# Two key loads cut at partition 68, longer rows of wo, and the last value sums behind the last scores, in a decode kernel on one core

## The chip, the cores and the metric

The kernel runs on one core of a Trainium2 chip. The metric is the device time of one execution in microseconds (us); of several executions the median is quoted. A comparison always uses a new kernel and the kernel before on the same chip in the same rounds.

## The reference, cut to what matters

One token (`x`, 640 values) passes a layer with attention over a long cache and a small feed-forward part.

```python
H, Sk, Dh = 32, 32768, 192
q = (layernorm(x) @ wq).reshape(1, 1, H, Dh)
scores = einsum("bhqd,bhkd->bhqk", q, k_cache) * Dh ** -0.5
p = softmax(scores)
o = einsum("bhqk,bhkd->bhqd", p, v_cache)
h = x + o.reshape(1, 1, H * Dh) @ wo
out = h + relu(layernorm(h) @ w1) @ w2
```

Keys and values are 2 x 32 x 32768 x 192 bf16 numbers, 805 MB, and each is used once. The rest is small: 825 MB are read in all.

## The kernel before

Keys and values come in 130 loads each. A usual load puts 64 keys on each of the 128 partitions: 128 rows of 24,576 bytes. The last head ends with short loads (40, 16 and 8 keys per partition, numbers 127, 128 and 129). All loads are issued from one queue, into three buffers for keys and three for values.

```python
def load_part(ld, src, pool, tag, name):
    h, k0, jl = loads[ld]
    ...
    t = pool.tile([P, size], bf16, tag=tag, name=name)
    nc.sync.dma_start(out=t[:, 0:jl * Dh],
                      in_=src[h, k0:k0 + P * jl, :].rearrange("(p j) d -> p (j d)", p=P))
    return t

wo_view = A_wo.rearrange("(b p) n -> p b n", p=P)
def load_wo(pr):                                   # once for each pair of heads
    t = wop.tile([P, 3, D], bf16, name="wo")
    nc.sync.dma_start(out=t[:], in_=wo_view[:, 3 * pr:3 * pr + 3, :])   # rows of 1280 bytes
```

Each load is worked on in chunks (32 keys per partition in the usual case). Of a chunk, TensorE transposes 20 keys per partition and forms their scores (`transposes`, `scores_pe`); VectorE does the other 12 with a multiplication and a sum (`scores_dve`); ScalarE takes the exponentials (`pB` and `pA`). The sum over values, `pv`, is a row of matmuls with `pA` or `pB` as weights. It runs one chunk later, behind the next chunk's transposes, so that TensorE has work while ScalarE copies the transposed keys.

```python
for g in range(G):
    ...                                            # issue loads
    transposes(g)
    if g > 0:
        pv(g - 1)
    scores_pe(g)
    sc = scores_dve(g)
    ...                                            # once per head: den, o_scale, o_turn, project, next q
    exp_dve(g, sc)
den_mm(H - 1); den_rec(H - 1)
pv(G - 1)
o_scale(H - 1); o_turn(H - 1); project(H // 2 - 1)
...                                                # layernorm, feed-forward, store
```

`o_scale` divides a head's sums by the softmax denominator, and `o_turn` puts two heads' results on partitions with 12 instructions on TensorE (six f32 matmuls, each recorded as two):

```python
nc.tensor.matmul(ps[:, b:b + 1], lhsT=src[:, i, b * P:(b + 1) * P], rhs=ident_f[0:2, i:i + 1], ...)
```

The softmax here doesn't subtract the row's maximum and nothing guards it: scores larger than these inputs give would overflow.

## Time and profile before

| kernel before | |
|---|---|
| time, median of 3 | 1954.45 us (1954.04 to 1954.61) |
| DMA bytes and mean rate | 827.85 MB, 424 GB/s |
| TensorE, VectorE, ScalarE busy | 82%, 69%, 55% |
| one 24,576-byte row on one DMA engine | 912 ns |
| 159 instruction fetches (queue q8) | spread over eight of the 16 engines by the prediction's count, 1.42 us lost in the one that was followed |

The lines that carry this stand in the prediction. To read them: the row of nines is the mean busy share of the 16 DMA engines in 40 slices of the span, and the row below it is what they moved. Both are flat until the last slice, so the stream of loads sets the time. The waits view of the kernel before says the same from the other side (columns: waiting engine, tile and line, what it waited for, us in total, times, longest):

```profile
DVE pr L266 <- DMA kt<-in_A_k_cache_dram: 479.9, 126, 8.8
PE tp L239 <- DMA kt<-in_A_k_cache_dram: 269.7, 119, 5.4
```

### The profile page before, as it was taken

How to read it: one execution, taken by the hardware profiler on the slowest of the kernel's cores; microseconds unless marked ns; L12 is line 12 of the kernel's file. 1: busy time of each engine (PE TensorE's matmuls, PEld its weight loads, DVE VectorE, ACT ScalarE, POOL GpSimd, SP SyncE). 2: the span in 40 equal slices, each digit the busy share in tenths (PEclk: the TensorE clock that was granted, in tenths of full speed). 3: DMA queues.
4: the chain of work that ended last, by engine and by line, in shares of the span. 5: the costliest groups of instructions: out<-in, count | busy, mean ns of one | idle time of the engine just before them, and what ended most of it. 6: DMA issues, size and time to landing. Idle time of an engine off the chain costs nothing.

```text
span 1952.3 us, 44906 instructions
## 1 busy us (share of the span) xinstructions
PE 1594.4 (82%) x20392; PEld 1122.4 (57%) x20392; DVE 1338.0 (69%) x654; ACT 1067.5 (55%) x2223; POOL 0.7 (0%) x6
## 2 busy tenths in 40 slices
PE   6887887878788788787888877888788887887887
PEld 4655565555556556555555655655555565565655
DVE  5766777667666676676767666777666766676675
ACT  4555555555555555555655555555555555555554
POOL 0000000000000000000000000000000000000000
PEclk9989889989998889998988989899899989898998
DMA  9999999999999999999999999999999999999996
GB/s 405 431 429 429 430 431 430 429 429 431 431 430 428 430 431 430 431 429 431 430 429 430 429 431 430 430 431 424 431 431 428 425 421 431 427 430 426 430 421 253
DMA packets 51522, 827.85 MB, mean 424 GB/s; under 512 B 4612, under 2 KB 17412, under 8 KB 18564
## 3 DMA queue, kind: packets, MB, share of 16 engines
q1 hardware_dynamic: 51332, 824.99, 99.0%
q8 instruction: 159, 2.61, 0.5%
q14 instruction: 31, 0.25, 0.0%
HBM read 824.97 MB, written 0.00 MB: 423 GB/s over the span
## 4 chain that ended last, share of the span: by engine, by line
DMA 77%; PE 17%; ACT 4%; DVE 1%; issue 1%; SPq 0%; ACTq 0%
DMA kt<-in_A_k_cache_dram 75%; PE o_ps L293 8%; PE tp L239 6%; ACT kT L240 3%; DMA vt<-in_A_v_cache_dram 1%; DVE pr L266 1%; PE sp L249 1%; PE sp L253 1%; PE sp L251 1%; PE qps L205 0%; ACT pA L276 0%; ACT pB L256 0%; DVE o_pair L314 0%; PE oT_ps L327 0%; ACT row_e L208 0%
## 5 line engine op out<-in xcount | busy, mean ns | idle before, releaser
L240 ACT COPY kT<-tp 128x1024 bf16<-128x1024 bf16 (+1 forms) x1025 | 905.2, 966 | 343.1 <-PE tp L239 340.2
L266 DVE TENSOR_TENSOR pr<-kt,qb 128x2304 f32<-128x2304 bf16 (+1 forms) x258 | 655.0, 2539 | 483.3 <-DMA kt<-in_A_k_cache_dram 479.9
L239 PE MATMUL tp<-ident_b,kt 128*128 128x128 bf16 x7677 | 599.3, 242 | 342.8 <-DMA kt<-in_A_k_cache_dram 269.7
L239 PEld LDWEIGHTS <-kt 128*128 128x128 bf16 x7677 | 531.1, 110 | 381.2 <-DMA kt<-in_A_k_cache_dram 280.2
L269 DVE TENSOR_REDUCE sc<-pr 128x12 f32<-128x2304 f32 (+1 forms) x258 | 654.3, 2536 | 27.6 <-ACT kT L240 1.4
L293 PE MATMUL o_ps<-vt,pB 128*2 128x384 bf16 x2559 | 498.8, 346 | 2.6 <-DMA vt<-in_A_v_cache_dram 2.6
L293 PEld LDWEIGHTS <-pB 128*2 128x2 bf16 x2559 | 203.8, 87 | 226.9 <-issue 65.9
L256 ACT ACTIVATE pB<-sp 128x20 bf16<-128x20 f32 (+1 forms) x258 | 48.4, 188 | 492.4 <-PE sp L253 492.4
L293 PE MATMUL o_ps<-vt,pA 128*2 128x384 bf16 x1537 | 291.9, 326 | 0.0
L249 PEld LDWEIGHTS <-kT 128*128 128x128 bf16 x2559 | 196.1, 96 | 85.7 <-issue 84.7
L249 PE MATMUL sp<-qm,kT 128*128 128x2 bf16 x2559 | 218.6, 164 | 0.5 <-ACT kT L240 0.5
L251 PE MATMUL sp<-qm,kT 128*128 128x1 bf16 x2559 | 215.0, 163 | 0.0
L253 PE MATMUL sp<-qm,kT 128*128 128x1 bf16 x2559 | 215.0, 163 | 0.0
L251 PEld LDWEIGHTS <-kT 128*128 128x128 bf16 x2559 | 198.7, 96 | 0.0
L293 PEld LDWEIGHTS <-pA 128*2 128x2 bf16 x1537 | 129.1, 84 | 120.8
L253 PEld LDWEIGHTS <-kT 128*128 128x128 bf16 x2559 | 197.4, 96 | 0.0
L276 ACT ACTIVATE pA<-sc 128x12 bf16<-128x12 f32 (+1 forms) x258 | 52.8, 205 | 0.0
L256 ACT ACTIVATION_READ_ACCUMULATOR pB<-sp 128x1 f32 x258 | 50.1, 194 | 0.0
L276 ACT ACTIVATION_READ_ACCUMULATOR pA<-sc 128x1 f32 x258 | 49.3, 191 | 0.0
L305 DVE TENSOR_REDUCE rec<-den 128x1 f32<-128x20 f32 x32 | 5.7, 179 | 60.2 <-PE den L299 60.2
L315 ACT ACTIVATE o_pair<-o_ps,rec 2x192 f32<-2x192 f32 x32 | 13.2, 412 | 26.9 <-DVE o_pair L314 26.9
L327 PE MATMUL oT_ps<-ident_f,o_pair 2*128 2x1 f32 x192 | 24.2, 247 | 0.1
(60 smaller groups left out, 191.4 us busy)
## 6 DMA issues: line engine op xcount, KB each, us to landing
kt<-in_A_k_cache_dram SPq DMA_DIRECT2D x127, 3072.0 KB, 35.7
vt<-in_A_v_cache_dram SPq DMA_DIRECT2D x127, 3072.0 KB, 31.4
wq<-in_A_wq_dram SPq DMA_DIRECT2D x8, 960.0 KB, 34.7
wo<-in_A_wo_dram SPq DMA_DIRECT2D x16, 480.0 KB, 31.2
kt<-in_A_k_cache_dram SPq DMA_DIRECT2D x1, 1920.0 KB, 30.7
vt<-in_A_v_cache_dram SPq DMA_DIRECT2D x1, 1920.0 KB, 25.4
kt<-in_B_w_dram SPq DMA_DIRECT2D x1, 1920.0 KB, 17.1
vt<-in_B_w_dram SPq DMA_DIRECT2D x2, 960.0 KB, 13.3
```

The lines of the kernel that those rows point to most:

```text
L239: nc.tensor.transpose(out=tp[:, b, :], in_=kt[:, off:off + P], identity=ident_b[:])
L240: nc.scalar.copy(out=kT[:, b0:b0 + nb, :], in_=tp[:, 0:nb, :])
L249: nc.tensor.matmul(sp[:, 2 * i:2 * i + 2], lhsT=kT[:, 3 * i + 1, :], rhs=qm[:, 1:3], start=True, stop=False, skip_group_check=True)
L251: nc.tensor.matmul(sp[:, 2 * i:2 * i + 1], lhsT=kT[:, 3 * i, :], rhs=qm[:, 0:1], start=False, stop=False, skip_group_check=True)
L253: nc.tensor.matmul(sp[:, 2 * i + 1:2 * i + 2], lhsT=kT[:, 3 * i + 2, :], rhs=qm[:, 3:4], start=False, stop=True, skip_group_check=True)
L256: nc.scalar.activation(out=pB[:, 0:JP], in_=sp[:, 0:JP], func=F.Exp, scale=SCALE, accum_out=dsums[:, h, 2 * c + 1:2 * c + 2])
L266: nc.vector.tensor_tensor(out=pr[:, 0:JD, :], in0=kt[:, c0 * Dh:(c0 + JD) * Dh].rearrange("p (j d) -> p j d", d=Dh), in1=qb[:].unsqueeze(1 ...
L269: nc.vector.reduce_sum(out=sc[:, 0:JD], in_=pr[:, 0:JD, :], axis=mybir.AxisListType.X)
L276: nc.scalar.activation(out=pA[:, 0:JD], in_=sc[:, 0:JD], func=F.Exp, scale=SCALE, accum_out=dsums[:, h, 2 * c:2 * c + 1])
L293: nc.tensor.matmul(o[:], lhsT=p, rhs=vt[:, (c0 + j) * Dh:(c0 + j + 2) * Dh], start=first, stop=last)
L315: nc.scalar.activation(out=dst[:, 1, n0:n0 + Dh], in_=o[:, Dh:2 * Dh], func=F.Copy, scale=s[0:2, 1:2])
L327: nc.tensor.matmul(ps[:, b:b + 1], lhsT=src[:, i, b * P:(b + 1) * P], rhs=ident_f[0:2, i:i + 1], start=(i == 0), stop=(i == 1))
```

## The change

Its intent, as the change itself suggests it: eight DMA engines are some 20 us behind the other eight at the end, as by the prediction's count they also carry the instruction fetches (1.42 us lost in the one that was followed). So it moves rows from engines 4 to 15 to engines 0 to 3 in two loads (60 and 117), makes the rows of `wo` three times longer, and takes the last value sums out of the way of the last scores.

```diff
+    few = (15 * len(loads) // 32, 29 * len(loads) // 32)
+    ENDS = [g for g in range(G) if chunks[g][2] >= len(loads) - NEND]
-    pcp = ... bufs=3
+    pcp = ... bufs=6
-    wo_view = A_wo.rearrange("(b p) n -> p b n", p=P)
+    wo_view = A_wo.rearrange("(g p b) n -> g p b n", p=P, b=3)
-        nc.sync.dma_start(out=t[:], in_=wo_view[:, 3 * pr:3 * pr + 3, :])
+        nc.sync.dma_start(out=t[:], in_=wo_view[pr])
-        nc.sync.dma_start(out=t[:, 0:jl * Dh], in_=src[h, k0:k0 + P * jl, :].rearrange(...))
+        rows = src[h, k0:k0 + P * jl, :].rearrange("(p j) d -> p (j d)", p=P)
+        for j0, j1 in parts or [(0, jl)]:
+            for p0, p1 in [(0, 68), (68, P)] if ld in few and name == "kt" else [(0, P)]:
+                nc.sync.dma_start(out=t[p0:p1, j0 * Dh:j1 * Dh], in_=rows[p0:p1, j0 * Dh:j1 * Dh])
...   (the value loads of the last head's end pass parts: one transfer per chunk)
-                    nc.tensor.matmul(ps[:, b:b + 1], lhsT=src[:, i, b * P:(b + 1) * P], ...)
+                    nc.tensor.matmul(ps[:, b:b + 1], lhsT=src[:, i, b:3 * P:3], ...)
-            if g > 0:
+            if g > 0 and g - 1 not in ENDS:
                 pv(g - 1)
...
         den_rec(H - 1)
-        pv(G - 1)
+        for g in ENDS:
+            pv(g)
```

More of the change, by code (lines that the diff above doesn't have):

```diff
@@ L79 @@
     scp = ctx.enter_context(tc.tile_pool(name="scp", bufs=3))
-    pcp = ctx.enter_context(tc.tile_pool(name="pcp", bufs=3))
+    pcp = ctx.enter_context(tc.tile_pool(name="pcp", bufs=6))
     small = ctx.enter_context(tc.tile_pool(name="small", bufs=2))
@@ L112, in load_wo, with load_part @@
         t = wop.tile([P, 3, D], bf16, name="wo")
-        nc.sync.dma_start(out=t[:], in_=wo_view[:, 3 * pr:3 * pr + 3, :])
+        nc.sync.dma_start(out=t[:], in_=wo_view[pr])
         wo_t[pr] = t
-    def load_part(ld, src, pool, tag, name):
+    def load_part(ld, src, pool, tag, name, parts=None):
         h, k0, jl = loads[ld]
@@ L122, in load_part @@
         t = pool.tile([P, size], bf16, tag=tag, name=name)
-        nc.sync.dma_start(out=t[:, 0:jl * Dh], in_=src[h, k0:k0 + P * jl, :].rearrange("(p j) d -> p (j d)", p=P))
+        rows = src[h, k0:k0 + P * jl, :].rearrange("(p j) d -> p (j d)", p=P)
+        for j0, j1 in parts or [(0, jl)]:
+            for p0, p1 in [(0, 68), (68, P)] if ld in few and name == "kt" else [(0, P)]:
+                nc.sync.dma_start(out=t[p0:p1, j0 * Dh:j1 * Dh], in_=rows[p0:p1, j0 * Dh:j1 * Dh])
         return t
@@ L129, in load_v @@
     def load_v(ld):
-        vt_t[ld] = load_part(ld, v_hd, vpool, "vt", "vt")
+        parts = [(q[3], q[3] + q[4]) for q in chunks if q[2] == ld] if ld >= len(loads) - NEND else None
+        vt_t[ld] = load_part(ld, v_hd, vpool, "vt", "vt", parts)
     w_t = {}
@@ L326, in o_turn @@
                 for i in range(2):
-                    nc.tensor.matmul(ps[:, b:b + 1], lhsT=src[:, i, b * P:(b + 1) * P], rhs=ident_f[0:2, i:i + 1],
+                    nc.tensor.matmul(ps[:, b:b + 1], lhsT=src[:, i, b:3 * P:3], rhs=ident_f[0:2, i:i + 1],
                                      start=(i == 0), stop=(i == 1))
```

## The prediction

> **What bounds the kernel now.** I read the page first (parts 2, 3, 4, 6), then the sync queue's and TensorE's lines of the timeline at the end, then the single DMA packets and semaphore landings that the trace keeps.
>
> ```profile
> span 1952.3 us, 44906 instructions
> DMA  9999999999999999999999999999999999999996
> GB/s 405 431 429 429 430 431 430 429 429 431 431 430 428 430 431 430 431 429 431 430 429 430 429 431 430 430 431 424 431 431 428 425 421 431 427 430 426 430 421 253
> q1 hardware_dynamic: 51332, 824.99, 99.0%
> q8 instruction: 159, 2.61, 0.5%
> ...
> DMA 77%; PE 17%; ACT 4%; DVE 1%; issue 1%; SPq 0%; ACTq 0%
> ...
> kt<-in_A_k_cache_dram SPq DMA_DIRECT2D x127, 3072.0 KB, 35.7
> ...
> wo<-in_A_wo_dram SPq DMA_DIRECT2D x16, 480.0 KB, 31.2
> ```
>
> The row of 9s and the flat 430 GB/s say that the transfers run without a pause until the last slice; the chain puts 77% on DMA. TensorE is busy 82% of the span but waits for keys (the waits view gives 269.7 us of it at the transposes). So only two things can move the time: the DMA stream, or the last 40 us after it.
>
> The stream has a grain that the page doesn't show. In the packet records a 24,576-byte row occupies an engine for 912 ns, and its successor starts 4 ns before its end: 908 ns a row, 27.1 GB/s, times 16 is 433 GB/s. So every engine runs at its pace all the time. But the 16 engines don't finish a load together. From the landings of each load, sorted: at 109 us eight landings are within 0.8 us of the first and eight are 1.7 to 1.8 us late; at 920 us (load 61) eight are 12.9 to 14.6 us late; from 1350 us on they are some 20 us late, and the gap stops growing. Of the early eight, six agree within 1.1 us, one is 1 to 4 us late, one 4 to 8.
>
> The cause is in the packets of q8: 159 instruction fetches of 16,384 bytes. Following rows of equal phase shows that they fall on eight engines in a fixed rotation. One example, 22.5 us into the span: the fetch takes 932 ns, in which its engine carries no row, and the next row takes 1411 ns instead of 912; the engine loses 1.42 us. 159/8 = 19.9 fetches per engine x 1.42 = **28.2 us** for each of eight engines; the gap's growth (14 us in 910 us, so 29 over 1924) agrees. A load is finished by its latest engine, so these eight set the time. The gap stays at 20 us since the early ones run out of issued loads.
>
> **The end.**
>
> ```profile
> 1893.43 12.61 SPq L123 DMA_DIRECT2D kt<-in_A_k_cache_dram  x3
> 1906.10 13.78 SPq L123 DMA_DIRECT2D vt<-in_A_v_cache_dram  x3
> ...
> 1912.12 3.38 PE L239 MATMUL tp<-ident_b,kt 128*128 128x128 bf16 x30 [3.39 <-DMA kt<-in_A_k_cache_dram]
> ...
> 1931.56 1.14 PE L293 MATMUL o_ps<-vt,pB 128*2 128x384 bf16 x6 [0.76 <-DMA vt<-in_A_v_cache_dram]
> ...
> 1937.27 0.97 PE L293 MATMUL o_ps<-vt,pB 128*2 128x384 bf16 x5
> ...
> 1939.51 0.40 PE L299 MATMUL den<-dsums,ones_mat 128*128 128x20 f32 x2 [0.54 <-ACT pA L276]
> 1939.84 0.49 PE L293 MATMUL o_ps<-vt,pB 128*2 128x384 bf16 x2
> ```
>
> The last real wait for the stream is the one for load 126, at 1912.1 (3.39 us). From there TensorE and ScalarE work through six chunks one after the other, with a single wait of 0.76 us for values. Loads 127, 128 and 129 of the keys are on the chip by 1924.1, 1926.0 and 1927.0, their values by 1931.5, 1933.4 and 1934.4. The value sums end at 1940.66, and 11.6 us of small steps follow.
>
> [...]
>
> **The change, part by part.**
>
> *68/60 split, key loads 60 and 117 (15/32 and 29/32 of 130).* Usual share 8 rows per engine. New: engines 0 to 3 get 17+4 = 21 (+13), 4 to 14 get 4 (-4), 15 gets none (-8). Over two loads: +26 rows on 0 to 3 = +23.6 us, -8 rows = -7.3 us on 4 to 14. This makes sense if engines 0 to 3 carry no fetches and the eight late ones lie in 4 to 15. I infer that from the change's numbers, since 23.6 against 28.2-7.3 = 20.9 is nearly a balance; the trace can't confirm it. Then the end is set by engines 0 to 3: 28.2-23.6 = **4.6 us earlier**. On the way: at load 60 they lead by 14 us and lose 17 rows = 15.4 us against the late ones, so they fall 1.5 us behind them; by load 117 they lead by 11.5 and fall 4 behind. That is far inside the 20 us of queue.
>
> *wo rows.* Per engine and load, 24 packets of 1280 bytes become 8 of 3840. Start to start 1280 takes 51.8 ns; 3840, between 3072 (121 recorded) and 6144 (234), about 149-4 = 145 ns. 24 x 51.8 = 1.24 us against 8 x 145 = 1.16; times 16 loads = **1.3 us earlier**. The strided ident matmuls (6 per pair of heads) I take as free.
>
> *Last scores first.* Chunks A, B (load 127), C, D lose their value sums from between the scores and get them after the denominator. Worked in the times of before: scores of A end at 1929.8; ScalarE's copies for B end at 1932.55, and the scores of B needn't wait for A's sums: exponentials at 1933.1 instead of 1933.9. C: copies 1933.7 to 1935.5, exponentials from 1936.0 (was 1936.95). D: its copy ends 1937.3, exponentials to 1938.05 (was 1939.46), denominator to 1938.5. Then all 10+10+8+4 = 32 sums stand behind it, at 1.78 us for ten: 5.3 us, to 1943.8, where they ended at 1940.66. So this costs **3.1 us**: it takes sums out of time in which TensorE waited for ScalarE, to avoid a wait for values of 0.76 us. The load of v 127 in two parts and pcp with 6 buffers gain nothing, as all values have landed by then.
>
> Sum: -4.6 - 1.3 + 3.1 = -2.8 us: 1951.6; I say 1951.
>
> **Rivals.**
> - [...] the 19 us that 21 rows take become up to 38, twice: engines 0 to 3 would then end up to 33 us after the present end (23.6+38-28.2): about 1988[...]. [...] Against: nothing in the trace; an amount so near a balance looks tuned by measurement.
> - *Wrong engines.* If one of the eight with fetches is among 0 to 3, it keeps 28.2 and gets 23.6: 1954.45+23.6-1.3+3.1 = 1980. [...] (the early engine that is up to 8 us late, some 10 by the end): 23.6+10-28.2 = +5.4, so 1962.
> - *The new order doesn't cost*, if the clock or ScalarE lets TensorE run the sums sooner than I think: 1948 to 1949.
> - *More from the stream:* if the latest engine loses all of its 7.3 us: also 1948 to 1949.
>
> **Range and chances.** Half of my weight is on 1947 to 1954, some 15% below it or in small variants, a third on contention or wrong engines, spread over 1955 to 1990. So 1944 to 1977 for 8 in 10. Faster by over 2% (below 1915) is out of the stream's reach; slower by over 2% (above 1993) needs full contention: 4%.
>
> **What would show it.** Right: the sorted landings of load 60 have four late engines, within 3 us of the other late ones; the gap of the eight is near zero after it, grows to some 11 us by load 117 and ends within 4 us; load 126 lands near 1906; TensorE then runs 32 sums in a row of 5.3 us behind the denominator, ending 3 us later after load 126's landing than now. Wrong: rows over 912 ns in number around load 60 (contention), or gaps of over 20 us after it (wrong engines), with TensorE waiting for keys in the middle of the run.

The sum: -4.6 - 1.3 + 3.1 = -2.8 us, 1951.6, said as 1951. Its first term supposes that 68 rows go to four engines and 60 rows to fifteen. The first rival, called contention in what follows, supposed that rows of different engines get in each other's way, so that one takes up to twice its time.

## The result, and the profile after

| | kernel before | changed kernel |
|---|---|---|
| time, median of 4 | 1954.24 us (1953.99 to 1954.61) | 2028.53 us (2026.11 to 2030.18) |
| ratio, 95% interval | | 1.0379 (1.0361 to 1.0397) |

The changed kernel is 3.8% slower.

The page of the changed kernel, its span, DMA rows, queue and key loads (the last group: tile and source, queue, operation, count, KB each, us from issue to landing):

```profile
span 2025.8 us, 44915 instructions
...
DMA  9999999999999999999999999999999999998994
GB/s 406 431 430 429 430 430 430 428 430 432 430 431 430 429 431 430 430 371 270 428 431 430 426 429 430 431 431 429 429 431 431 425 430 429 431 228 311 431 404 170
...
q1 hardware_dynamic: 47386, 824.99, 97.9%
...
kt<-in_A_k_cache_dram SPq DMA_DIRECT2D x125, 3072.0 KB, 35.4
...
kt<-in_A_k_cache_dram SPq DMA_DIRECT2D x2, 1440.0 KB, 73.9
```

The last line is the 60-row part of the cut loads: 73.9 us from issue to landing, where a usual key load takes 35.4. The bytes are the same as before, the packets fewer (47,386 against 51,332: longer `wo` rows). What is new is in two places of the GB/s row, around 900 us and 1800 us, where the two cut loads are: 371 and 270, then 228 and 311, in place of 430. And the row of nines above doesn't move at the first of them. **The engines are as busy as ever and move half as much.** The engine shares alone would have hidden it.

The size of the loss can be read off that row. A slice is 2025.8/40 = 50.6 us. Against 430 GB/s the slices of 371 and 270 lose 50.6 x (59 + 160)/430 = 25.8 us, and those of 228 and 311 lose 50.6 x (202 + 119)/430 = 37.8 us: 64 us together, of the 74 that the kernel got slower.

A closer look: the windows view of the kernel before, then of the changed kernel, around the first cut load (columns: stretch, length, busy time and instructions of each engine, TensorE's granted clock, DMA share, GB/s):

```profile
890.00:898.50 8.50, 8.50 (x104) 6.54 (x102) 8.26 (x4) 5.15 (x11) 0.00 (x0) 0.81 1.01 433
898.50:905.50 7.00, 4.37 (x59) 2.63 (x56) 1.63 (x1) 3.68 (x10) 0.00 (x0) 1.00 0.99 424
```

```profile
890.00:898.50 8.50, 8.24 (x97) 5.79 (x95) 8.26 (x4) 5.52 (x12) 0.00 (x0) 0.80 1.05 424
898.50:905.50 7.00, 4.20 (x57) 2.56 (x56) 1.24 (x1) 3.25 (x9) 0.00 (x0) 1.00 1.01 211
...
915.00:930.00 15.00, 9.19 (x86) 5.04 (x84) 5.91 (x3) 4.22 (x9) 0.00 (x0) 0.80 1.05 204
930.00:943.00 13.00, 1.27 (x32) 0.86 (x30) 0.00 (x0) 0.47 (x4) 0.00 (x0) 0.63 0.97 206
```

The rate falls at 898.5 us, at once, and stays at half for some 45 us, at a DMA share near 1. In the DMA records no row that starts between 899 and 942 us takes under 1665 ns, and the median of these 357 rows is 1854. The last columns are the ones to compare; in the last stretch the compute engines have run out of keys.

The waits view of the changed kernel:

```profile
DVE pr L274 <- DMA kt<-in_A_k_cache_dram: 529.8, 115, 39.5
PE tp L247 <- DMA kt<-in_A_k_cache_dram: 303.4, 112, 31.5
```

These are 49.9 us and 33.7 us more than before, in fewer waits, and the longest grew from 8.8 to 39.5 us: the new wait sits in one or two places.

Following the landings of single loads against the kernel before: the values of load 58 land at about the same time (0.4 us sooner), load 60 is complete 29.9 us late, the delay has shrunk to 22 us by load 115, is 70 us when load 117 is complete, 67 to 68 us for the last values, and 73 us at the output. So each cut costs tens of microseconds, and the end costs another five. At the second cut there is more: when the slow rows are through, the engines have nothing left to do, since the computation had starved and freed no buffers. The windows view of the changed kernel shows it as a share below one:

```profile
1830.00:1840.00 10.00, 0.00 (x0) 0.00 (x0) 0.00 (x0) 0.00 (x0) 0.00 (x0) 0.50 0.76 307
1840.00:1850.00 10.00, 3.12 (x30) 3.12 (x30) 3.02 (x2) 2.01 (x3) 0.00 (x0) 0.50 0.58 236
```

TensorE's timeline at the end of the changed kernel (start, length, engine, line, operation, tiles, shapes, count, idle time before and its releaser), to be held against the tail in the prediction:

```profile
2004.61 0.62 PE L307 MATMUL den<-dsums,ones_mat 128*128 128x20 f32 x2 [0.54 <-ACT pA L284]
2005.16 2.08 PE L301 MATMUL o_ps<-vt,pB 128*2 128x384 bf16 x6
2007.03 1.48 PE L301 MATMUL o_ps<-vt,pA 128*2 128x384 bf16 x4
...
2012.16 0.49 PE L301 MATMUL o_ps<-vt,pA 128*2 128x384 bf16 x2
```

The value sums do stand in one row behind the denominator, as planned. But the first six take 2.08 us, where six took 1.14 us in the kernel before, and the row lasts from 2005.16 to 2012.65, 7.5 us instead of the 5.3 that the prediction had worked out.

### The profile page after: what moved, and what is told of

It is laid out like the page before. It is cut to its first block, busy times and chain, and to the rows that moved or that the text cites. A ratio compares the mean times of both kernels' runs of the same rounds, so it can differ in the third digit from the quotient of the medians.

```text
span 2025.8 us, 44915 instructions
## 1 busy us (share of the span) xinstructions
PE 1619.3 (80%) x20392; PEld 1137.7 (56%) x20392; DVE 1336.9 (66%) x654; ACT 1067.3 (53%) x2223; POOL 0.7 (0%) x6
## 3 DMA queue, kind: packets, MB, share of 16 engines
q1 hardware_dynamic: 47386, 824.99, 97.9%
## 4 chain that ended last, share of the span: by engine, by line
DMA 73%; PE 18%; ACT 4%; another core or an unknown queue 2%; DVE 2%; issue 1%; SPq 0%; ACTq 0%
DMA kt<-in_A_k_cache_dram 68%; PE o_ps L301 9%; PE tp L247 6%; DMA vt<-in_A_v_cache_dram 5%; ACT kT L248 3%; DVE pr L274 1%; PE sp L257 1%; PE sp L261 1%; PE oT_ps L335 1%; PE sp L259 1%; DVE o_pair L322 0%; ACT pA L284 0%; ACT pB L264 0%; PE den L307 0%
## 5 line engine op out<-in xcount | busy, mean ns | idle before, releaser
L301 PE MATMUL o_ps<-vt,pB 128*2 128x384 bf16 x2559 | 508.7, 350 | 13.1 <-DMA vt<-in_A_v_cache_dram 13.0
L335 PE MATMUL oT_ps<-ident_f,o_pair 2*128 2x1 f32 x192 | 36.4, 312 | 0.5 <-DVE o_pair L322 0.5
L335 PEld LDWEIGHTS oT_ps<-ident_f,o_pair 2*128 2x128 f32 x192 | 35.0, 258 | 1.2 <-DVE o_pair L322 0.9
## 6 DMA issues: line engine op xcount, KB each, us to landing
kt<-in_A_k_cache_dram SPq DMA_DIRECT2D x125, 3072.0 KB, 35.4
kt<-in_A_k_cache_dram SPq DMA_DIRECT2D x2, 1440.0 KB, 73.9
vt<-in_A_v_cache_dram SPq DMA_DIRECT2D x2, 960.0 KB, 23.6
```

The lines of the kernel that those rows point to most:

```text
L301: nc.tensor.matmul(o[:], lhsT=p, rhs=vt[:, (c0 + j) * Dh:(c0 + j + 2) * Dh], start=first, stop=last)
L335: nc.tensor.matmul(ps[:, b:b + 1], lhsT=src[:, i, b:3 * P:3], rhs=ident_f[0:2, i:i + 1], start=(i == 0), stop=(i == 1))
```

## The experiments

All kernels are the kernel before with one edit, except "no_split", which is the changed kernel with one edit, and "wo_perm" and "parts_wo", which join two. All gave correct results. The "two theories" of the expectations are contention and overloaded engines (too many rows on engines 0 to 3). "Rows" are the durations of 24,576-byte packets in the trace's DMA records.

| run | what it does | median us | ratio to before (95%) |
|---|---|---|---|
| no_split | the change without the cut loads | 1958.97 | 1.0022 (1.0009 to 1.0036) |
| split_only | the cut loads alone | 2021.91 | 1.0347 (1.0332 to 1.0361) |
| wo_only | the wo rows alone | 1954.66 | 1.0000 (0.9987 to 1.0012) |
| order_only | the new order alone | 1959.23 | 1.0023 (1.0011 to 1.0036) |
| halves_64 | the two loads cut at partition 64 | 1996.91 | 1.0216 (1.0199 to 1.0233) |
| columns | the two loads cut along the row | 1955.15 | 1.0001 (0.9986 to 1.0016) |
| markers | 16 tiny transfers, to number the engines | 1955.77 | one run |
| spread | the cut in small doses | 2010.99 | 1.0286 (1.0271 to 1.0302) |
| block16 | eight transfers of 16 neighbouring rows | 1990.18 | 1.0182 (1.0168 to 1.0195) |
| stride16 | eight transfers of every eighth row | 1985.13 | 1.0156 (1.0142 to 1.0170) |
| own8 | eight-row transfers, each engine in its usual partitions | 1974.29 | 1.0100 (1.0085 to 1.0116) |
| foreign8 | the same, each engine in partitions of another | 1991.95 | 1.0185 (1.0170 to 1.0200) |
| dram_perm | full width, rows read elsewhere in memory | 1954.82 | 0.9999 (0.9982 to 1.0015) |
| wo_perm | long wo rows, no strided weights | 1954.59 | 1.0001 (0.9989 to 1.0014) |
| order_warm | the new order, TensorE kept busy | 1956.72 | 1.0011 (0.9997 to 1.0025) |
| parts_wo | wo_perm and the end's values in parts | 1953.63 | 0.9989 (0.9975 to 1.0003) |

The medians of the kernel before in the same rounds lay between 1954.34 and 1955.07.

### Which part of the change costs the time

**no_split** sets the list of cut loads to nothing:

```diff
-    few = (15 * len(loads) // 32, 29 * len(loads) // 32)
+    few = ()
```

> The changed kernel with the 68/60 split alone taken out (wo rows and late value sums stay). If the split carries the loss [...], the 74 us vanish and what is left is the rest of the change: -1.3 us for wo, +3.1 us for the order, so 1956 us and the last key load lands as before. If the late value sums cost much more than I worked out, 1960 us or more.

**split_only** puts the cut alone into the kernel before:

```diff
+        if name == "kt" and ld in (60, 117):
+            for p0, p1 in [(0, 68), (68, P)]:
+                nc.sync.dma_start(out=t[p0:p1, 0:jl * Dh], in_=rows[p0:p1, 0:jl * Dh])
```

> The kernel before with the 68/60 split of key loads 60 and 117 alone. Both theories: some 2022 to 2027 us, with the landings of load 60 delayed by 30 us and rows of 1.8 and 2.7 us around it. If the split needs the other parts to do harm, less than 2000 us.

Measured: 1958.97 (4.3 us above the kernel before of its rounds, 1954.65) and 2021.91 (67.3 above). Together 71.6, of the 74.3 that the whole change costs; 2.7 us are not put down to either, but the four runs of split_only lie between 2019.77 and 2026.98, so these 2.7 us are not clear of noise. So the cut loads are the cause, and their delay is there in split_only at the same loads: 30.2 us at load 60 and 68.0 at load 117, measured at the landing of each.

### Wrong engines, or slow rows

The prediction's two serious rivals were that engines 0 to 3 are not the early ones, and that the rows get slow. **markers** sends one tiny transfer of n rows for each n from 1 to 16 in the middle of the run; each has n landings. The trace has no engine numbers, so an engine is numbered here by the first of these transfers that lands on it: the landing that is new with each n belongs to engine n-1. That the 68 rows of a cut load go to the first four of this numbering is an assumption, but it fits: in the changed kernel they are through at 931.6, 931.9, 936.8 and 942.4 us, two together and two later, as engines 0 and 2, then 3 and 1 are below.

```diff
+    marks = [const.tile([16, 16], bf16, name=f"mark{n}") for n in range(1, 17)]
+    def mark(n):
+        nc.sync.dma_start(out=marks[n - 1][0:n, :], in_=A_wo[0:n, 0:16])
...
+            if 16 <= h < 20 and c in (2, 3, 5, 6):
+                mark(4 * (h - 16) + {2: 1, 3: 2, 5: 3, 6: 4}[c])
```

> The kernel before with 16 tiny transfers of 1 to 16 rows of 32 bytes, four in each of heads 16 to 19, to learn engine numbers: a transfer of n rows lands on n engines, each when its queue gets there. [...] engines 0 to 3 are early ones (the transfers of 1 to 4 rows land early, 14 us or more ahead of the late eight), so the loss isn't from fetches on them. Wrong engines: at least one of the first four landings is 13 us or more late. Time as before within 2 us.

Engines 0, 2, 7, 8 and 15 are the early ones. Behind them, 4 is 1.0 to 1.9 us late, 3 is 3.3 to 4.4 and 1 is 5.6 to 7.3; why, no run shows. The eight late ones, 14 to 19 us, are 5, 6 and 9 to 14. So the prediction's inference that none of the eight is among engines 0 to 3 was right, and the first rival falls in its main form. Its milder form, an engine among the four that is up to 8 us late, holds: that is engine 1.

The rows decide for the second. Durations of all rows that start between 900.5 and 904.5 us, from the DMA records (not a view of the profile):

```
kernel      rows   shortest  median  longest (ns)
before        70        912     912       912
after         38       1766    1866      2446
split_only    35       1752    1865      2088
halves_64     33       1636    1942      2329
own8          55        912     912       912
foreign8      31       1833    1876      1922
block16       35       1718    1780      2007
stride16      33       1849    1924      1991
```

Twice the time per row, and not only on engines 0 to 3. At that moment the early engines have reached the cut load. The eight late ones, 14 us behind, are still on the loads before it, with 128 partitions as always, and one engine, 15 by this numbering, has no row of the cut load at all (fifteen landings for the 60 rows, and the four of the 68 rows are among them: 938.8, 939.2, 944.1 and 950.0 us, 7.2 to 7.6 us after the first four). **Every one of their rows is slow too**; the shortest in the changed kernel and in split_only is 1752 ns.

### What about the cut makes rows slow

**halves_64** cuts at 64, which gives every engine its usual number of rows, 4 + 4, if 64 rows go to 16 engines as 128 do (16 landings for a usual load). **columns** cuts each row in two, which makes two transfers as well, but both on 128 partitions. The 1.8 us a row in the expectation of halves_64 are twice the usual 908 ns, an assumption. The 5 ns for a packet in that of columns are an estimate: a 1280-byte packet takes 51.8 ns from start to start in the kernel before, and 1280 bytes at 27.1 GB/s alone would take 47.2.

```diff
+            for p0, p1 in [(0, 64), (64, P)]:                        # halves_64
+                nc.sync.dma_start(out=t[p0:p1, 0:jl * Dh], in_=rows[p0:p1, 0:jl * Dh])
```
```diff
+            for c0 in (0, jl * Dh // 2):                             # columns
+                nc.sync.dma_start(out=t[:, c0:c0 + jl * Dh // 2], in_=rows[:, c0:c0 + jl * Dh // 2])
```

> The kernel before, key loads 60 and 117 as two transfers of 64 rows, each on 16 engines, 4 rows each. No engine gets more than its 8 rows. [...] rows of 1.8 us, 7.3 us longer per load, 10 to 15 us slower in all. Overloaded engines (the amount of rows on engines 0 to 3 alone does it): no difference within 0.5 us, rows stay at 912 ns.

> Control for halves_64: the same two loads as two transfers of 128 rows with half of the columns each, so twice the transfers [...]. Both theories: within 0.5 us of before (8 more packets per engine and load, at some 5 ns each). If it is the cutting in two that costs, as slow as halves_64.

The windows views of halves_64 and then of columns:

```profile
898.50:905.50 7.00, 5.01 (x70) 3.24 (x67) 1.77 (x1) 4.32 (x11) 0.00 (x0) 1.00 1.04 221
```

```profile
898.50:905.50 7.00, 6.74 (x102) 5.04 (x102) 2.87 (x2) 5.37 (x15) 0.00 (x0) 1.00 1.02 435
```

Two transfers in place of one cost nothing. A cut across the partitions costs 42 us for two loads even where no engine gets more rows: the unequal counts are not the cause, at most they make it last longer. Contention had been reckoned at 10 to 15 us here, so its reach was underrated by some three times. The rest of the way from halves_64 (42.2 us) to split_only (67.3) presumably comes with the 21 rows of the four loaded engines; no run separates it.

**spread** tests whether small doses would be absorbed. It moves about the same bytes from late to early engines, but with the last 8 keys per partition of 15 loads (120 keys where two whole loads have 128):

```diff
+        if name == "kt" and ld % 8 == 4 and ld < 124:
+            c1 = (jl - 8) * Dh
+            nc.sync.dma_start(out=t[:, 0:c1], in_=rows[:, 0:c1])
+            for p0, p1 in [(0, 68), (68, P)]:
+                nc.sync.dma_start(out=t[p0:p1, c1:jl * Dh], in_=rows[p0:p1, c1:jl * Dh])
```

> The kernel before; in 16 of the key loads the last 8 of 64 row groups go by the 68/60 split, the other 56 by 128 rows: the same bytes moved between engines as in two whole loads, in 16 small doses. If only engine totals matter and the harm came from the size of the dose: a gain of some 4.6 us, 1950 us. [...] each dose delays the late engines by up to 1.5 us (the 12 us before load 60, over 8), 10 to 25 us slower in all.

It takes 2010.99 us, 56 us above the kernel before and more than the 10 to 25 expected, and the page of spread shows a dent in many slices in place of two deep ones:

```profile
GB/s 404 416 429 409 429 430 408 429 406 431 430 404 429 404 429 429 403 425 403 425 430 399 422 403 429 418 411 424 402 427 413 414 423 405 426 417 412 428 427 192
```

The loss goes with the bytes that are written in this way, not with one long blockage that a queue could hide.

### Neighbouring partitions, or partitions of another engine

Half speed is 204 to 221 GB/s in the windows above, and it is the rate of all 16 engines, also of those that are on other loads. What about the partitions brings it on, these views don't tell: the DMA records have neither engine nor partition. The author assumed that an engine always writes the same partitions in a load of 128 rows, and calls all others foreign to it. Which partitions these are no trace here shows; "owner" and "foreign" stand for that assumption.

**block16** and **stride16** ask whether it matters how close to each other 16 engines write (the 16-row transfer of markers has 16 landings). A transfer of block16 takes 16 neighbouring rows, one of stride16 every eighth row. That a row takes four times as long in the first and twice in the second was the author's assumption.

```diff
+                nc.sync.dma_start(out=t[16 * i:16 * i + 16, 0:jl * Dh], in_=rows[16 * i:16 * i + 16, :])   # block16, i = 0..7
+                nc.sync.dma_start(out=t[i:P:8, 0:jl * Dh], in_=rows[i:P:8, :])                            # stride16, i = 0..7
```

> The kernel before, key loads 60 and 117 each as eight transfers of 16 neighbouring rows, one row per engine and transfer. Every engine moves its usual 8 rows. [...] the typical row of these loads takes 4 x 908 = 3.6 us; each load some 22 us longer by itself and more by the second meeting of early and late engines: 80 us or more slower in all. If it is only that the cutting in parts or a wrong owner costs[...]: as slow as stride16.

> As block16 (eight transfers of 16 rows, one per engine, the same bytes, sizes and counts), but each takes every eighth partition. [...] rows of 1.8 us, as in halves_64, some 42 us slower in all, half of what block16 loses or less. If the number of transfers or rows on foreign engines decides [...]: the same time as block16.

1990.18 and 1985.13 us: 36 and 31 us above the kernel before, not the 80 and 42 expected. The 5 us between them are clear of noise (the four runs of each don't overlap), but small, and the rows of the table above are nearly alike, 1780 and 1924 ns in the median. Between 918 and 926 us the slowest tenth of block16's rows starts at 2497 ns and that of stride16's at 1872, so closeness may matter for some. As the engines don't go through the eight transfers in step (eight are some 14 us behind), how many wrote close to each other at one time isn't known. This pair doesn't settle it. Nor are the totals pure: eight small transfers for one load also hold up the issue of the next (in own8, below, they take 32 us to issue).

**own8** and **foreign8** are the sharper pair. Both start the load with eight transfers of eight rows, one row to an engine (the 8-row transfer of markers has eight landings). In own8 they go to partitions 0 to 63, in foreign8 in the same pattern to 64 to 127. By the assumption each engine thus writes its own partitions in own8 and foreign ones in foreign8. Counts and bytes are the same. Then one transfer brings the other 64 rows.

```diff
+            for o in (0, 1, 2, 3, 32, 33, 34, 35):
+                nc.sync.dma_start(out=t[o:o + 29:4, 0:jl * Dh], in_=rows[o:o + 29:4, :])                  # own8
+            nc.sync.dma_start(out=t[64:128, 0:jl * Dh], in_=rows[64:128, :])
```
```diff
+                nc.sync.dma_start(out=t[64 + o:64 + o + 29:4, ...], in_=rows[64 + o:64 + o + 29:4, :])    # foreign8
+            nc.sync.dma_start(out=t[0:64, ...], in_=rows[0:64, :])
```

> The kernel before; key loads 60 and 117 as eight transfers of 8 rows (every fourth partition of 0 to 63, by engines 0 to 7[...]), then the other 64 rows in one transfer on 16 engines. If writing foreign partitions halves the rates: the rows of the first eight transfers take 912 ns and all engines stay at 431 GB/s for some 7 us after the first engine gets there, until it reaches the 64-row transfer; less loss than foreign8. If any transfer that isn't 128 rows wide does it: half rate at once, and the same loss as foreign8.

> As own8 with the halves exchanged: first eight transfers of 8 rows of partitions 64 to 127, again by engines 0 to 7[...]; then rows 0 to 63 in one transfer. Foreign partitions: half rate for all engines from the first row, and about 7 us per load more lost than in own8. Width or number of engines: no difference from own8.

The windows views of own8 and then of foreign8:

```profile
898.50:905.50 7.00, 4.42 (x60) 2.65 (x57) 1.79 (x1) 3.73 (x10) 0.00 (x0) 1.00 0.81 343
905.50:915.00 9.50, 8.82 (x107) 6.40 (x108) 8.79 (x4) 5.55 (x10) 0.00 (x0) 0.82 0.48 188
915.00:930.00 15.00, 4.88 (x60) 3.38 (x60) 2.78 (x2) 2.70 (x8) 0.00 (x0) 0.68 0.99 244
```

```profile
898.50:905.50 7.00, 5.66 (x81) 3.89 (x79) 1.82 (x1) 4.97 (x14) 0.00 (x0) 1.00 0.89 197
```

Read the last two columns together. own8 moves 343 GB/s at a share of 0.81, and 343/0.81 = 423: full speed on those engines that have work. foreign8 moves 197 at 0.89, which is 221 at full share: half speed. The rows say it directly: all 55 of own8 take 912 ns, those of foreign8 1876 in the median. Half speed comes to own8 only in the third line (244 GB/s), with its 64-row transfer.

So **the same eight small transfers leave all rows at 912 ns in partitions 0 to 63 and double them in 64 to 127**, and a transfer isn't slow because it is narrow, small, strided or cut. Nor are partitions 0 to 63 fast as such: the first transfer of halves_64 writes just these, and the rows in flight take 1942 ns in the median. Rows that are slow while engines write foreign partitions, in which the owners are writing too, would fit all of this, but that is the author's reading: which engine writes what isn't in any trace. own8 and foreign8 end 18 us apart, of some 14 expected (7 for each load). own8 isn't free all the same, 20 us above the kernel before, partly through that 64-row transfer and partly since small transfers hold up the queue. The sync queue's timeline of own8:

```profile
881.33 32.27 SPq L126 DMA_DIRECT2D kt<-in_A_k_cache_dram  x8
```

Its eight issues take 32 us, mostly as the queue waits for earlier transfers to land (13.8 us for keys, 13.1 for values), and in the second line of its windows the share falls to 0.48.

**dram_perm** checks the other end of the transfer. It keeps 128 partitions and reads the rows from other places in memory, as two halves per partition:

```diff
+            nc.sync.dma_start(out=t[:, 0:jl * Dh].rearrange("p (a x) -> p a x", a=2),
+                              in_=src[h, k0:k0 + P * jl, :].rearrange("(a p j) d -> p a (j d)", a=2, p=P))
```

> The kernel before; key and value loads 60 and 117 read 128 rows wide, each partition from two pieces of 12288 bytes 1.5 MB apart instead of one of 24576, so that the order of reads in HBM changes [...] (keys and values are permuted alike, so the result stays right). Partitions as the cause: within 0.5 us of before. Reads in HBM as the cause: rates fall around these loads, 10 us or more.

Nothing changes (0.9999), so this change in the order of reads does no harm, and what is left is the side that is written.

### The tail: order and clock

**order_only** is the new order with its six buffers:

```diff
-            if g > 0:
+            if g > 0 and g - 1 not in ENDS:
                 pv(g - 1)
-        pv(G - 1)
+        for g in ENDS:
+            pv(g)
```

> The kernel before with the value sums of the last four chunks behind the denominator alone (values loaded whole, 6 buffers). Worked out: 3.1 us slower, 1957.4 us, the 32 sums in one row of 5.3 us. Rival, that the clock or ScalarE lets the scores come earlier: 0 to 1.5 us slower; rival, that the clock falls there: 5 us or more slower.

It costs 4.6 us, where the prediction had worked out 3.1. TensorE's timeline at the end of order_only, and two stretches of its windows:

```profile
1938.80 2.08 PE L294 MATMUL o_ps<-vt,pB 128*2 128x384 bf16 x6
1940.67 1.33 PE L294 MATMUL o_ps<-vt,pA 128*2 128x384 bf16 x4
1941.84 1.14 PE L294 MATMUL o_ps<-vt,pB 128*2 128x384 bf16 x6
1942.81 0.81 PE L294 MATMUL o_ps<-vt,pA 128*2 128x384 bf16 x4
```

```profile
1934.00:1938.20 4.20, 1.68 (x27) 1.25 (x27) 2.06 (x3) 3.09 (x11) 0.00 (x0) 0.60 0.92 334
1938.20:1942.00 3.80, 3.75 (x14) 1.81 (x15) 0.34 (x2) 0.00 (x0) 0.00 (x0) 0.54 0.53 191
```

From the start of its first sum to the end of its last, the same ten sums take 3.20 us in the first chunk (1938.80 to 1942.00) and 1.78 in the second. The column ahead of the DMA share suggests the reason: with its value sums taken away, TensorE is busy for 1.68 of 4.20 us, its granted clock falls to 0.60, and it is still at 0.54 when the sums come. 3.20 - 1.78 = 1.4 us, about the difference between 4.6 and 3.1. From 1942.0 to 1945.5 us it is at 1.00 again.

**order_warm** tests that: it puts six useless matmuls where each value sum stood.

```diff
+            elif g > 0:
+                idle = ops.tile([2, 2 * Dh], f32, tag="o_ps", name="idle")
+                for _ in range(6):
+                    nc.tensor.matmul(idle[:], lhsT=ident_b[:, 0:2], rhs=kt_t[ld][:, 0:2 * Dh], start=True, stop=True)
```

> order_only with six idle matmuls of 384 columns after the transposes of each of the last chunks, where TensorE only waits for ScalarE. Theory: of the 4.6 us that order_only costs, 3.1 are the sums out of their gaps and 1.5 a granted clock of 0.54 to 0.60 after a stretch with little for TensorE to do; kept busy, the clock stays at 1.0 and the time falls to some 1957.7 us. Rival, that all of it is the order: 1959 us or more.

TensorE's timeline of order_warm at the same point, and one stretch of its windows:

```profile
1937.56 1.14 PE L294 MATMUL o_ps<-vt,pB 128*2 128x384 bf16 x6
1938.53 0.81 PE L294 MATMUL o_ps<-vt,pA 128*2 128x384 bf16 x4
```

```profile
1938.20:1942.00 3.80, 3.80 (x26) 1.99 (x24) 0.00 (x0) 0.00 (x0) 0.00 (x0) 1.00 0.53 198
```

The clock stays at 1.00, the sums run at the usual pace and start 1.2 us sooner. order_warm is 2.4 us above the kernel before of its rounds, where order_only was 4.6 above that of its own: 2.2 us come back, somewhat more than the 1.4 us of the ten sums, as the steps ahead of them ran at the low clock (0.60) too. The 2.4 us that remain are the price of the order itself, or a little more than it, as the useless matmuls may cost something. The interval just reaches 1 (0.9997), but the five runs (1956.01 to 1957.25) all lie above the nine of the kernel before (1954.10 to 1955.92).

### The longer rows of wo

**wo_only** is that part alone, with the strided weights of `o_turn`. **wo_perm** has the same rows, but stores the scaled results in the order needed, so that the weights are contiguous:

```diff
+            put = [dst[:, i, :].rearrange("q (b p) -> q p b", b=3)[:, p0:p0 + P // 2, :] for i in range(2)]
+            got = [o[:, i * Dh:(i + 1) * Dh].rearrange("q (p b) -> q p b", b=3) for i in range(2)]
+            nc.vector.tensor_scalar_mul(out=put[0], in0=got[0], scalar1=s[0:2, 1:2])
```

> The kernel before with 3840-byte wo rows alone. Worked out: 1.3 us faster, 1953.0 us (the landings before load 53 of the changed kernel came 0.6 us earlier after 7 wo loads, which fits). If small packets cost nothing beside the stream: no difference, within 0.3 us.

> wo rows of 3840 bytes as in wo_only, but the scaled outputs are written in the permuted order, so that the f32 weight loads of the 12 small matmuls are contiguous again. Theory: wo_only's stream was 1.1 us earlier and lost it because strided f32 weight loads took 322 instead of 186 ns and waited for both heads; here the matmuls go back to 245 ns, and 0.5 to 1 us of gain is left: 1953.7 to 1954.2 us. Rival, that the loss of wo_only was the clock or chance: no different from wo_only.

Both are equal to the kernel before. The stream of wo_only does end 1.1 us sooner (load 126 lands at 1911.0 instead of 1912.1), and its value sums 1.1 us sooner, at 1939.5. The 12 instructions of the last `o_turn` give it back. The view of that tile in the last microseconds, before and then wo_only (shortest/median/longest ns):

```profile
L327 PEld LDWEIGHTS oT_ps<-ident_f,o_pair x12: 181/186/187, 1940.6 to 1942.1; 2*128 2x128 f32 x12
L327 PE MATMUL oT_ps<-ident_f,o_pair x12: 245/245/266, 1940.6 to 1942.2; 2*128 2x1 f32 x12
```

```profile
L327 PEld LDWEIGHTS oT_ps<-ident_f,o_pair x12: 248/322/325, 1940.0 to 1942.3; 2*128 2x128 f32 x12
L327 PE MATMUL oT_ps<-ident_f,o_pair x12: 309/347/368, 1940.0 to 1942.4; 2*128 2x1 f32 x12
```

The weights are read with a stride of three, and a load of them takes 322 ns instead of 186. Also, each block now holds results of both heads, so the first can't start on the earlier head's while the later one is scaled. TensorE's timeline for the 12 of the kernel before, and then of wo_only:

```profile
1940.58 1.84 PE L327 MATMUL oT_ps<-ident_f,o_pair 2*128 2x1 f32 x12
```

```profile
1940.01 2.73 PE L327 MATMUL oT_ps<-ident_f,o_pair 2*128 2x1 f32 x12 [0.50 <-DVE o_pair L314]
```

They start 0.57 us sooner and end 0.3 us later. wo_perm takes the stride away (245 ns again), but the wait for both heads stays, and so does the time; in its profiled run the stream was only 0.5 to 0.6 us sooner at the end.

### A version to beat both

**parts_wo** joins wo_perm to the remaining part of the change, the values of the end in one transfer per chunk, with the order of before:

```diff
+        parts = [(q[3], q[3] + q[4]) for q in chunks if q[2] == ld] if ld >= len(loads) - NEND else None
+        vt_t[ld] = load_part(ld, v_hd, vpool, "vt", "vt", parts)
```

> A version meant to beat both: the kernel before with 3840-byte wo rows and contiguous weight loads (as wo_perm), and the load of v 127 in two parts, so that TensorE's 0.76 us wait for values goes; sums in their old places, no 68/60 split. Worked out: 1.1 us from the stream less up to 1 us that the small matmuls wait for both heads, and up to 0.7 us from the wait: 1953.4 to 1954.2, at the edge of what five rounds resolve. Rival: ScalarE's copies bound that stretch anyway, and nothing is gained: 1954.6.

1953.63 us against 1955.07 in its rounds, a ratio of 0.9989 with an interval up to 1.0003. It is 3.7% under the changed kernel, and not shown to be faster than the kernel before.

## Why the prediction was wrong

**Right.** The bound and its grain: the stream sets the time, and all rows of the kernel before took 912 ns at that point. Eight engines are late, and none of engines 0 to 3 is among these eight (markers). The transfers go to as many engines as supposed: the 68 rows have four landings, the 60 rows fifteen. The stream's gain from longer `wo` rows was 1.1 us in wo_only and 0.5 to 0.6 in wo_perm, of 1.3 predicted. The direction of the new order was right too.

**The step that failed** is the first term of the sum: "engines 0 to 3 get 17+4 = 21 (+13)", and "Over two loads: +26 rows on 0 to 3 = +23.6 us, -8 rows = -7.3 us on 4 to 14", which made the end 4.6 us earlier. It gives a row 908 ns wherever it is written. In the cut loads it takes about 1850, and so does every other row in flight. The cut alone costs 67.3 us in place of gaining 4.6.

The same term also takes engines 0 to 3 as one early block, and they aren't: engine 1 is 5.6 to 7.3 us late in markers. By the prediction's own milder rival (+5.4 us) the cut would then have made the end some 5 us later even at 908 ns a row. That is an estimate; no run has the cut without the slow rows.

The reason given for trusting that step was that "an amount so near a balance looks tuned by measurement". The balance is real, and it is a balance of row counts; it says nothing of how long such a row takes. A tidy sum in a change is no evidence that its author has timed it.

**The rival that came nearest** was contention. Its factor was right: "the 19 us that 21 rows take become up to 38", and rows did double. Its reach was too small: its sum slowed engines 0 to 3 alone. In fact all 16 are slow from the first engine's entry into the cut load until engines 0 to 3 have written its 68 rows (the last at 942.4 us), some 45 us at the first cut. At (430 - 207)/430 of lost rate that is 45 x 0.52 = 23 us, and 22 us is the delay that remains before the second cut. With 33 us at most for it, where the two cuts cost 67, and a chance of 4% for more than 2% slower, the range ended far below what came.

**Two terms were mis-sized.** For the order, 3.1 us became 4.6, as the granted clock fell to 0.60 and 0.54 when the value sums were gone from between the scores (order_warm, with a full clock, pays 2.4). For `wo`, -1.3 became 0.0, as the strided matmuls that I took "as free" took 2.73 us instead of 1.84, on the path that sets the end. (One sum of the prediction has a slip: 32 sums "at 1.78 us for ten" would be 5.7 us, not 5.3. The 5.3 itself is sound: at full clock, in order_warm, the row takes 5.4 us, from 1937.56 to 1942.92.)

**What stays open.** own8 and foreign8 show that the same small transfers halve the rate in partitions 64 to 127 (1876 ns a row) and not in 0 to 63 (912). That foreign partitions are the cause is the reading, and no run isolates an engine that writes such partitions while their owner writes elsewhere, so the foreign partition as such and the meeting of two engines in it aren't separated. Why it also slows engines on usual loads, no run here shows. Open as well, if they are more than noise, are the 2.7 us by which the parts' sum falls short.

The second cut costs more than the first: its load lands 70 us late, 48 us more than the 22 before it, where the first cost 30. The landings show much of the reason. The four engines finish its 68 rows at 1817.3, 1819.4, 1821.3 and 1839.5 us (931.6, 931.9, 936.8 and 942.4 at the first cut), so the last of them is alone. At load 120 fifteen engines land within 1.7 us of the first and one 19.4 us after it, and at load 126 it is still 19.8 us (the others at most 3.0): **one engine sets the end of the stream**, most likely engine 1, the latest of the four in markers. The others run out of issued loads while they wait for it; the share of 0.76 and 0.58 from 1830 us on is (0.24 + 0.42) x 10 = 6.6 us of that. In halves_64, where no engine gets more rows, the two cuts cost alike (20.5 us at load 115, 40.3 at the values of load 117).

## What to carry to other kernels

Cut a large load along its rows, not across the partitions: beside this kernel's stream the first cost nothing (1.0001), while cuts across at 64 and 68 halved the rate of everything in flight (221 and 211 GB/s, of 430). When a kernel is bound by its transfers, read the DMA share and the GB/s together, for a share of 1.0 at half the GB/s was a slow path here, not idle engines. And before taking work out of a TensorE gap near the end, see what the granted clock does without it (0.60 and 0.54 here, in place of 1.00).
